# Attention tiles merged in shared PSUM banks, TensorE ordered by hand, a padded half tile and an unsplit kept relu in an attention and mixer kernel

## Chip, cores and metric

The kernel runs on one core of one Trainium2 chip. The metric is device time in microseconds from start to end of one execution. Engines: TensorE (PE) multiplies and writes only to PSUM, an accumulator memory of eight banks per partition; VectorE (DVE) and ScalarE (ACT) read PSUM and work elementwise; GpSimd (POOL) works on SBUF alone; SyncE (SP) issues the DMA transfers. A matmul has a stationary operand, loaded by its own instruction (PEld), and a moving one.

## The reference

```python
scores = scale * np.matmul(q_c, k_c.transpose(0, 1, 2, 4, 3))      # 8 x 8 heads, 9 chunks of 64, head size 64
scores = scores - np.max(scores, axis=-1, keepdims=True)
attn = np.exp(scores)
attn = attn / (np.sum(attn, axis=-1, keepdims=True) + 1e-09)
out = np.matmul(attn, v_c)
...
h = np.maximum(xt @ w_tok1, 0.0) @ w_tok2      # x: 8 batches, 576 x 512; 576 -> 256 -> 576 along the sequence
u = x + h.transpose(0, 2, 1)
h2 = np.maximum(u @ w_ch1, 0.0) @ w_ch2        # 512 -> 1536 -> 512 along the channels
return (u + h2).astype(np.float32)
```

Attention is over chunks of 64 positions. Its output, with the heads side by side, goes through a mixer: a two-layer token mix over the 576 positions, a sum, and a two-layer channel mix.

## The kernel before

**Precision.** The big products are made in a rounded form of float32. An operand is split into a high part (rounded, by ScalarE) and a low part (the rest, a subtraction), and a product is three matmuls: high by high, low weights by high, high weights by low (`THREE`). Weights arrive as raw 64-bit words; five VectorE operations and three ScalarE ones turn a block of 128x512 into its two parts (`conversion`, `split_high`, `split_low`; the result is named `kept_c1_f`, `kept_c2_f`, `kept_t...`).

**Tiles.** Two batches share nine attention tiles of 128 rows: the even batch has tiles 0 to 3 and the first half of tile 4, the odd one tiles 5 to 8 and the second half of tile 4. So an even batch attends five tiles, an odd one four. The half tile is stacked: its high part on 64 partitions and its low part on the other 64 (`attn_stack`).

**One attention tile.** `attn_s`: 16 matmuls of 64x64 in plain float32, each in two passes, so 32 in the trace, four running side by side in quarters of the array; `attn_p`: maximum and subtraction on VectorE, exponential on ScalarE; `attn_far`: transposition in blocks of 32 on VectorE, then through DRAM and back (`far`, `pf`); `attn_t`: a copy on ScalarE (`pt`); `attn_v`: 16 matmuls of 64x65 with the values, whose 65th column is all ones and gives the row sums; `attn_o`: reciprocal and product (`x`); `attn_end`: split into `xh` (ScalarE) and `xl` (GpSimd) and a second way through DRAM, whose landing in `xt` is `attn_x`. Scores and values each have the one pair of banks of `ps_at`, in turn.

**One batch of the mixer.** `tok1` (twice 14 matmuls of 128x512, of which one has 64 rows: the low weights of the half tile), its relu split into `rh` and `rl`; `tok2` (8 groups of 6 matmuls of 128x288) and the sum `u`, split into `uh` and `ul`; then for both halves of 288 columns twelve groups `ch1` (12 matmuls of 128x288, relu split into `gh` and `gl`) and twelve groups `ch2` (12 matmuls that add up in four banks, `acc`). A group of `ch2` follows the next group of `ch1`. At the end of a half the four sums are read by VectorE (`o`) and written out.

**Stages and order.** Up to about 36 us batch 0's attention runs, with PE, VectorE and ScalarE ordered by hand. Then batch 0's channel mix runs while the weights are converted: `ch1` for both halves, `ch2` for the first, the relu of the second kept split (`gh1`, `gl1`), and after it `ch2` of the second half. Batch 1's four attention tiles are placed in between by the table `JOBS`, whose slots count two per channel group. Then the main loop runs over batches 1 to 7; in batch b it attends the tiles of b+1, in pieces that a generator hands out one per channel group. In the last two stages the engines' orders are made when the program is built, by a simulated timeline with the written order as priority; only SyncE's is the written one throughout. Each engine's order is then fixed.

Of the kernel before, what the change touches and what calls it, by code (L numbers as in the profile page):

```python
# [60 lines left out]
def attention_mixer_kernel(ctx, tc, qk_in, v_in, w1_in, w2_in, wc1_in, wc2_in, out):  # L61
# [279 lines left out]
    def attn_o(i, fill=(0, 0)):  # L341
        t = tiles[i]
        pv = t["pv"]
        zi = pool.tile([P, 2, NHP, 1], F32, tag="zi", name="zi")
        nc.vector.tensor_scalar_add(out=zi, in0=pv[:, :, :, D:], scalar1=1e-9)
        convert(fill[0])
        nc.vector.reciprocal(out=zi, in_=zi)
        convert(fill[1])
# [327 lines left out]
    def jobs_of(b):  # L676
        if b >= B:
            return
        ts = batch_tiles(b)
        for j in range(len(ts) + 1):  # L680
            if j < len(ts):
                attn_s(ts[j])
                attn_p(ts[j])
                attn_far(ts[j])
                yield
                attn_t(ts[j])
            if j:
                attn_x(b, ts[j - 1])
            elif b % 2:
                attn_x(b, ts[0] - 1)  # L690
            yield
            yield
            if j < len(ts):
                attn_v(ts[j])
                attn_o(ts[j])
                attn_end(ts[j])
                if j + 2 < len(ts):
                    attn_load(ts[j + 2])
                elif b + 1 < B:
                    attn_load(batch_tiles(b + 1)[j + 2 - len(ts)])  # L700
            yield

    pend = None
    for b in range(1, B):
# [7 lines left out]
        jobs = jobs_of(b + 1)  # L712
        r = []
        for n in range(2):
            accs = []
            for f in range(NFC):
                g = ch1(us[n], f)
                end = n == 1 and f == NFC - 1
                if end:
                    for _ in jobs:  # L720
                        pass
                    if b + 1 < B:
                        r.append(tok1(b + 1, 0))
                else:
                    next(jobs, None)
# [60 lines left out]
```

## Time and profile before

| | us |
|---|---|
| three runs, median | 830.99 |
| lowest, highest | 830.38, 831.02 |
| the profiled execution | 831.2 |
| its span, first to last instruction | 829.4 |

| | busy us | share of the span |
|---|---|---|
| PE | 810.3 | 98% |
| PEld | 759.8 | 92% |
| DVE | 364.7 | 44% |
| ACT | 234.9 | 28% |
| POOL | 118.3 | 14% |

A line of a timeline has the start in us, the length in us, the engine, the line of the program, the operation and its operands with their shapes; "x12" stands for twelve instructions of a kind in a row, and a bracket at the end for idle time before the first and what ended it. A line of stretches has the stretch, its length, then busy time and instructions of PE, PEld, DVE, ACT and POOL, the clock that PE was granted, the share of busy DMA and the GB/s. A line of groups has line, engine, operation, operands and count, then total and mean time, then idle time before. Matmuls overlap, so the pace of PE is read from start to start.

### The profile page before, as it was taken

What the parts mean: (1) busy time and instruction counts of PE and PEld (TensorE: products, weight loads), DVE (VectorE), ACT (ScalarE), POOL (GpSimd) and SP (SyncE); (2) the same over time, 40 slices, a digit from 0 to 9 for tenths busy, and PEclk for the clock granted to TensorE, in tenths of its full rate; (3) what the DMA queues carried; (4) which work ended last, traced back from release to release, by engine and by line L of the source; (5) the groups of instructions that cost most, each with busy time, mean ns of one, the idle gap of its engine ahead of it and who ended that gap; (6) DMA issues with size and microseconds to landing.
All of it is one profiled execution on the core that took longest, in us unless ns stands there. A gap on an engine that the chain in (4) does not pass through costs nothing.

```text
span 829.4 us, 17900 instructions
## 1 busy us (share of the span) xinstructions
PE 810.3 (98%) x7556; PEld 759.8 (92%) x7556; DVE 364.7 (44%) x770; ACT 234.9 (28%) x484; POOL 118.3 (14%) x133
## 2 busy tenths in 40 slices
PE   7898999999999999999999999999999999999998
PEld 5578889999999999899998999999998999989998
DVE  5899993633335342343335334143433434223121
ACT  4676751322223221132223221132222322112110
POOL 0000021402103120220203102030200312014000
PEclk7999999999999999999999999999999999999999
DMA  9953232423442333023433233212353132200000
GB/s 352 407 188 102 91 103 67 144 96 96 133 121 86 120 121 122 29 75 106 131 103 99 99 113 119 65 55 90 98 162 109 62 101 92 93 24 6 1 30 29
DMA packets 69984, 87.96 MB, mean 106 GB/s; under 512 B 8016, under 2 KB 48208, under 8 KB 69904
## 3 DMA queue, kind: packets, MB, share of 16 engines
q1 hardware_dynamic: 69904, 86.82, 31.6%
q8 instruction: 59, 0.97, 0.5%
q14 instruction: 21, 0.17, 0.1%
HBM read 59.92 MB, written 25.95 MB: 104 GB/s over the span
## 4 chain that ended last, share of the span: by engine, by line
PE 88%; DVE 8%; DMA 1%; issue 1%; ACT 1%; SPq 0%; DVEq 0%; ACTq 0%
PE acc L516 36%; PE ps_c L487 34%; PE ps_t L466 6%; PE ps_t L428 6%; PE ps_s L262 3%; PE ps_v L333 2%; DVE wtop L165 1%; DVE wtop L173 1%; DVE kept_c L223 1%; DMA raw_t<-in_w 1%; DVE wtop L152 1%; DVE gl L495 1%; PE sum L437 1%; DVE wtop L158 1%; DVE mx L274 0%
## 5 line engine op out<-in xcount | busy, mean ns | idle before, releaser
L487 PE MATMUL ps_c<-uh,kept_c 128*128 128x288 f32 x1536 | 316.9, 297 | 3.4 <-ACT xt L399 1.9
L516 PE MATMUL acc<-gh,kept_c 128*128 128x288 f32 x1536 | 299.8, 297 | 0.9 <-ACT kept_c L217 0.9
L487 PEld LDWEIGHTS ps_c<-uh,kept_c 128*128 128x128 f32 x1536 | 247.2, 189 | 6.2 <-ACT xt L399 2.1
L516 PEld LDWEIGHTS acc<-gh,kept_c 128*128 128x128 f32 x1536 | 239.0, 188 | 4.5 <-ACT kept_c L217 1.1
L487 PE MATMUL ps_c<-ul,kept_c 128*128 128x288 f32 x768 | 227.8, 297 | 0.0
L495 DVE SCALAR_TENSOR_TENSOR gl<-ps_c,gh 128x288 fp32r<-128x288 f32 x192 | 87.3, 455 | 307.5 <-ACT gh L494 307.3
L516 PE MATMUL acc<-gl,kept_c 128*128 128x288 f32 x768 | 204.1, 297 | 0.0
L494 ACT ACTIVATE gh<-ps_c 128x288 fp32r<-128x288 f32 x192 | 78.9, 411 | 324.3 <-PE ps_c L487 313.3
L487 PEld LDWEIGHTS ps_c<-ul,kept_c 128*128 128x128 f32 x768 | 144.7, 189 | 0.6
L516 PEld LDWEIGHTS acc<-gl,kept_c 128*128 128x128 f32 x768 | 137.2, 189 | 1.2
L370 POOL TENSOR_TENSOR xl<-x,xh 128x512 fp32r<-128x512 f32 x28 | 36.8, 1314 | 387.8 <-ACT xh L369 387.8
L525 POOL TENSOR_TENSOR o<-o,ul 128x288 f32<-128x288 f32 x56 | 44.6, 828 | 228.9 <-DVE o L523 215.4
L466 PE MATMUL ps_t<-kept_t,rh 128*128 128x288 f32 x224 | 45.6, 301 | 0.4 <-ACT rh L445 0.4
L476 ACT CAST uh<-u 128x288 fp32r<-128x288 f32 x64 | 26.7, 432 | 46.2 <-DVE u L471 46.1
L274 DVE TENSOR_REDUCE mx<-ps_s 128x8 f32<-128x512 f32 x36 | 24.8, 688 | 29.4 <-PE ps_s L262 29.4
L466 PEld LDWEIGHTS ps_t<-kept_t,rh 128*128 128x128 f32 x224 | 35.2, 188 | 1.6 <-ACT rh L445 0.9
L314 ACT COPY pt<-pf 128x512 f32<-128x512 f32 x31 | 19.3, 622 | 60.3 <-DMA pf<-far 60.2
L428 PE MATMUL ps_t<-xh,kept_t 128*128 128x512 f32 x112 | 36.1, 403 | 0.0
L471 DVE TENSOR_TENSOR u<-ps_t,xt 128x288 f32<-128x288 f32 x64 | 28.0, 451 | 17.1 <-PE ps_t L466 16.0
L281 ACT ACTIVATE pr<-pr 128x512 f32<-128x512 f32 x36 | 22.8, 633 | 44.6 <-DVE pr L277 44.5
L477 POOL TENSOR_TENSOR ul<-u,uh 128x288 fp32r<-128x288 f32 x35 | 29.6, 855 | 20.5 <-ACT uh L476 20.1
L262 PEld LDWEIGHTS ps_s<-qk 64*64 64x64 f32 x1152 | 23.4, 138 | 9.8 <-issue 7.3
(61 smaller groups left out, 610.2 us busy)
## 6 DMA issues: line engine op xcount, KB each, us to landing
qk<-in_qk SPq DMA_DIRECT2D x36, 512.0 KB, 4.0
far<-blocks SPq DMA_DIRECT2D x63, 256.0 KB, 2.1
raw_c<-in_wc SPq DMA_DIRECT2D x24, 512.0 KB, 9.0
v<-in_v SPq DMA_DIRECT2D x36, 260.0 KB, 4.1
out<-o SPq DMA_DIRECT2D x64, 144.0 KB, 1.9
pf<-far SPq DMA_DIRECT2D x124, 64.0 KB, 2.0
xt<-far SPq DMA_DIRECT2D x112, 64.0 KB, 2.0
raw_t<-in_w SPq DMA_DIRECT2D x4, 288.0 KB, 7.6
```

What stands on the lines that cost most here:

```text
L262: nc.tensor.matmul(ps[c * CH:(c + 1) * CH, a, hp * CH:(hp + 1) * CH], lhsT=qk[a * D:(a + 1) * D, 0, hp, c * CH:(c + 1) * CH], rhs=qk[a * D ...
L370: nc.gpsimd.tensor_tensor(out=xl, in0=t["x"], in1=xh.bitcast(F32), op=ALU.subtract)
L428: nc.tensor.matmul(ps, lhsT=lhsT, rhs=rhs, start=(n == 0 and q == 0), stop=(n == len(mt) - 1 and q == len(terms) - 1),)
L466: nc.tensor.matmul(ps[:, :HALF], lhsT=lhsT[:, m * P:(m + 1) * P], rhs=rhs, start=(k == 0 and q == 0), stop=(k == NT1 - 1 and q == len(term ...
L471: nc.vector.tensor_tensor(out=u.rearrange("p (i c) -> p i c", c=BK), in0=ps[:, :HALF].rearrange("p (i c) -> p i c", c=BK), in1=xt[:, n * H ...
L476: nc.scalar.copy(out=uh[:, m], in_=u)
L477: return lambda engine: engine.tensor_tensor(out=ul[:, m], in0=u, in1=uh[:, m].bitcast(F32), op=ALU.subtract)
L487: nc.tensor.matmul(ps[:, :HALF], lhsT=weights["c1", f][:, wi, k * P:(k + 1) * P], rhs=u[ui][:, k], start=(k == 0 and q == 0), stop=(k == N ...
L494: nc.scalar.activation(out=gh, in_=ps[:, :HALF], func=AF.Relu)
L495: nc.vector.scalar_tensor_tensor(out=gl, in0=ps[:, :HALF], scalar=0.0, in1=gh.bitcast(F32), op0=ALU.max, op1=ALU.subtract)
L516: nc.tensor.matmul(accs[e], lhsT=weights["c2", f][:, wi, e * P:(e + 1) * P], rhs=g[gi], start=(f == 0 and q == 0), stop=(f == NFC - 1 and ...
L525: nc.gpsimd.tensor_tensor(out=o, in0=o, in1=u[1][:, e].bitcast(F32), op=ALU.add)
```

## The change

Four edits, and tables of numbers to go with them.

1. In the main loop the score matmuls of one tile and the value matmuls of the tile before it are issued together (`attn_both`), into the two halves of one pair of banks (`ps_sv`). The value matmuls leave out the column of ones; the row sums are now a reduction of the probabilities on VectorE (`attn_z`). `attention(k)` issues all of a step, and the steps stand at channel groups 19, 15, 11, 7 and 3 of a batch, or 19, 14, 9 and 4, with one more at group 0 of batch 1.
2. PE's order in the main loop is the written one (`manual_schedule`).
3. The half tile's low weights are kept in two copies of 128 rows, each zero in one half (`half_low`, made with `half_mask`), so that all matmuls of `tok1` have 128 rows. Batch 0's first token mix stays as it was.
4. The kept relu of batch 0's second half is one float32 tile (`g1`); it is split by a copy and a subtraction one group ahead of its use (`split_g`).

`JOBS` puts batch 1's attention two or more slots earlier and the split of the token weights two later, weights are fetched six blocks ahead instead of five, and three buffers hold low words instead of four.

```diff
-AHEAD = 5
+LAST_STEP, STRIDE, FIRST_STEP = 19, {5: 4, 4: 5}, 0
+AHEAD = 6
...
-STARTS = ((10, 11, 13, 14), (15, 16, 18, 19), (20, 21, 24, 25), (25, 27, 30, 31))
+STARTS = ((8, 9, 11, 12), (13, 14, 16, 17), (18, 19, 21, 22), (23, 24, 26, 27))
...
-JOBS += [(25 + i, "split", i) for i in range(7)]
+JOBS += [(27 + i, "split", i) for i in range(7)]
...
-        lows[i] = pool.tile([P, DM], I32, tag="low", name="low", bufs=4)[:, :n]
+        lows[i] = pool.tile([P, DM], I32, tag="low", name="low", bufs=3)[:, :n]
...
+    def attn_z(i):
+        t = tiles[i]
+        zi = t["zi"] = pool.tile([P, 2, NHP, 1], F32, tag="zs", name="zs")
+        nc.vector.tensor_reduce(
+            out=zi, in_=t["pr"].rearrange("p (h a k) -> p a h k", a=2, k=CH), axis=AX.X, op=ALU.add
+        )
+        nc.vector.tensor_scalar_add(out=zi, in0=zi, scalar1=1e-9)
+        nc.vector.reciprocal(out=zi, in_=zi)
+    def attn_both(i, j):
+        ps = ps_at.tile([P, 2, 512], F32, tag="at", name="ps_sv")
...
+                            ps[c * CH:(c + 1) * CH, a, hp * CH:(hp + 1) * CH],
+                            lhsT=qk[a * D:(a + 1) * D, 0, hp, c * CH:(c + 1) * CH],
+                            rhs=qk[a * D:(a + 1) * D, 1, hp, c * CH:(c + 1) * CH],
...
+                            ps[c * CH:(c + 1) * CH, a, (NHP + hp) * D:(NHP + hp + 1) * D],
+                            lhsT=t["pt"][a * CH:(a + 1) * CH, hp, c * CH:(c + 1) * CH],
+                            rhs=t["v"][a * CH:(a + 1) * CH, c, hp, :D],
...
-            terms = ((w[:, 0], st), (w[rows, 1], st[rows]))
+            terms = ((w[:, 0], st), (half_low[b % 2][:, m * P:(m + 1) * P], st))
...
+        if kept:
+            g = pool.tile([P, HALF], F32, tag="g1", name="g1", bufs=NFC)
+            nc.scalar.activation(out=g, in_=ps[:, :HALF], func=AF.Relu)
+            return g
...
+    def split_g(g):
+        gh, gl = g_parts()
+        nc.scalar.copy(out=gh, in_=g)
+        nc.vector.tensor_tensor(out=gl, in0=g, in1=gh.bitcast(F32), op=ALU.subtract)
+        return gh, gl
...
+        g, ahead = ahead, split_g(kept[f + 1]) if f + 1 < NFC else None
+        ch2(0, 1, us[1], f, g, accs)
...
+    def attention(k):
+        i = order[k] if k < len(order) else None
+        j = order[k - 1] if k else None
+        if j is not None:
+            attn_t(j)
+        attn_both(i, j)
+        if j is not None and k + 1 < len(order):
+            attn_load(order[k + 1])
+        if i is not None:
+            attn_p(i)
+            attn_far(i)
+            attn_z(i)
+        if j is not None:
+            attn_o(j)
+            attn_end(j)
...
+    by_hand.enter_context(tc.manual_schedule(engines={nc.tensor.engine}))
```

Three places in the built orders show what moved. Numbers behind names count the tiles of the program; a row stands for as many matmuls as its last "x" says.

PE in the main loop, before: the start of a batch's token mix (`ps_t2`), in which the scores of the next tile (`ps_s`) are spread.

```order
L262 MATMUL ps_s_8306<-qk_7800 64x64 x10
L466 MATMUL ps_t2_8199<-kept_t2_0_0_1999,rh_8134 128x288 x2
L466 MATMUL ps_t2_8199<-kept_t2_0_0_1999,rl_8135 128x288
L466 MATMUL ps_t2_8199<-kept_t2_1_0_2017,rh_8165 128x288 x2
L466 MATMUL ps_t2_8210<-kept_t2_0_0_1999,rh_8134 128x288 x2
L466 MATMUL ps_t2_8210<-kept_t2_0_0_1999,rl_8135 128x288
L466 MATMUL ps_t2_8210<-kept_t2_1_0_2017,rh_8165 128x288 x2
L262 MATMUL ps_s_8306<-qk_7800 64x64 x3
L466 MATMUL ps_t2_8199<-kept_t2_1_0_2017,rl_8166 128x288
L466 MATMUL ps_t2_8210<-kept_t2_1_0_2017,rl_8166 128x288
L262 MATMUL ps_s_8306<-qk_7800 64x64 x2
```

PE in the main loop, of the change: an attention step behind a `ch1` group (`ps_c1`) and ahead of a `ch2` group (`acc`).

```order
L535 MATMUL ps_c1_4373<-uh_3547,kept_c1_7_1215 128x288 x2
L535 MATMUL ps_c1_4373<-ul_3548,kept_c1_7_1215 128x288
L309 MATMUL ps_sv_4392<-qk_4209 64x64 x16
L321 MATMUL ps_sv_4392<-v_3975,pt_4390 64x64 x16
L575 MATMUL acc_4141<-gh_4357,kept_c2_6_1246 128x288 x2
L575 MATMUL acc_4141<-gl_4358,kept_c2_6_1246 128x288
```

Scores and values stand together and between whole groups. From the first `tok2` matmul of batch 1 on, PE has 71 runs of such small matmuls before and 28 of the change, with 864 small matmuls in both.

PE at the hand-over from batch 0 to the main loop, before: the last tile's values (`ps_v`), batch 1's token mix (`ps_t1`), a `ch2` group, and the end of the token mix, which needs the last tile (`xh_2074`, `xl_2075`).

```order
L333 MATMUL ps_v_2034<-v_1682,pt_2032 64x65 x16
L428 MATMUL ps_t1_2147<-xh_1411,kept_t1_0_2_1936 128x512
L428 MATMUL ps_t1_2147<-xl_1412,kept_t1_0_2_1936 128x512
...
L516 MATMUL acc_1847<-gh_1803,kept_c2_11_1664 128x288 x2
L516 MATMUL acc_1847<-gl_1804,kept_c2_11_1664 128x288
...
L428 MATMUL ps_t1_2116<-xh_2074,kept_t1_2_2_1954 128x512 x2
L428 MATMUL ps_t1_2147<-xh_2074,kept_t1_2_2_1954 128x512 x2
L428 MATMUL ps_t1_2116<-xl_2075,kept_t1_2_2_1954 128x512
```

The same place of the change.

```order
L575 MATMUL acc_1896<-gl_2165,kept_c2_11_1687 128x288
L575 MATMUL acc_1897<-gl_2165,kept_c2_11_1687 128x288
L379 MATMUL ps_v_1953<-v_1597,pt_1951 64x65 x16
L476 MATMUL ps_t1_2145<-xh_1991,kept_t1_2_2_2028 128x512 x2
L476 MATMUL ps_t1_2180<-xh_1991,kept_t1_2_2_2028 128x512 x2
L476 MATMUL ps_t1_2145<-xl_1992,kept_t1_2_2_2028 128x512
L476 MATMUL ps_t1_2180<-xl_1992,kept_t1_2_2_2028 128x512
L514 MATMUL ps_t2_2239<-kept_t2_0_0_2076,rh_2160 128x288 x2
```

The values and the token matmuls that need them now follow each other.

VectorE at the same hand-over, before: from batch 0's first four output sums (`o`) to the third tile's row sums (`zi`).

```order
L523 TENSOR_TENSOR o_1843<-acc_904,uh_669 128x288
L223 TENSOR_TENSOR kept_t1_0_2_1936<-wtop_257,kept_t1_0_2_1936 128x512
L223 TENSOR_TENSOR kept_t1_2_2_1954<-wtop_286,kept_t1_2_2_1954 128x512
L223 TENSOR_TENSOR kept_t1_4_1_1981<-wtop_354,kept_t1_4_1_1981 128x256
L223 TENSOR_TENSOR kept_t2_0_0_1999<-wtop_374,kept_t2_0_0_1999 128x288
L223 TENSOR_TENSOR kept_t2_1_0_2017<-wtop_379,kept_t2_1_0_2017 128x288
L223 TENSOR_TENSOR kept_t2_0_1_2059<-wtop_452,kept_t2_0_1_2059 128x288
L223 TENSOR_TENSOR kept_t2_1_1_2089<-wtop_457,kept_t2_1_1_2089 128x288
L345 TENSOR_SCALAR zi_1882<-ps_v_1865 128x8
```

Of the change: from the last tile's transpose (`blocks_1910`) to the low part of a relu of the second half (`gl_2165`).

```order
L332 STREAM_TRANSPOSE blocks_1910<-pr_1843 128x4x4x32
L231 TENSOR_TENSOR kept_t1_0_2_2006<-wtop_263,kept_t1_0_2_2006 128x512
L231 TENSOR_TENSOR kept_t1_2_2_2028<-wtop_292,kept_t1_2_2_2028 128x512
L231 TENSOR_TENSOR kept_t1_4_1_2050<-wtop_360,kept_t1_4_1_2050 128x256
L231 TENSOR_TENSOR kept_t2_0_0_2076<-wtop_380,kept_t2_0_0_2076 128x288
L231 TENSOR_TENSOR kept_t2_1_0_2098<-wtop_385,kept_t2_1_0_2098 128x288
L701 TENSOR_SCALAR half_low0_2053<-kept_t1_4_1_2050,half_mask_81 128x256
L701 TENSOR_SCALAR half_low1_2055<-kept_t1_4_1_2050,half_mask_81 128x256
L231 TENSOR_TENSOR kept_t2_0_1_2120<-wtop_458,kept_t2_0_1_2120 128x288
L231 TENSOR_TENSOR kept_t2_1_1_2142<-wtop_463,kept_t2_1_1_2142 128x288
L556 TENSOR_TENSOR gl_2165<-g1_1822,gh_2164 128x288
```

The seven low halves of the token weights stood ahead of the third tile's row sums. Now they stand, with the two masked copies, behind the last tile's transpose.

More of the change, by code (lines that the diff above doesn't have):

```diff
@@ L108, in warm @@
                 nc.tensor.matmul(ps[:, :HALF], lhsT=warm_in[:, :P], rhs=warm_in, start=True, stop=True)
+    half_mask = const.tile([P, 2], F32, name="half_mask")
+    for c in range(2):
+        nc.gpsimd.memset(half_mask[:, c:c + 1], 0.0)
+        nc.gpsimd.memset(half_mask[c * CH:(c + 1) * CH, c:c + 1], 1.0)
+    half_low = []
     weights, tops, lows = {}, {}, {}
@@ L343, in attn_o @@
         pv = t["pv"]
[L344 to L348, printed above, removed]
+        zi = t.get("zi")
+        if zi is None:
+            zi = pool.tile([P, 2, NHP, 1], F32, tag="zi", name="zi")
+            nc.vector.tensor_scalar_add(out=zi, in0=pv[:, :, :, D:], scalar1=1e-9)
+            convert(fill[0])
+            nc.vector.reciprocal(out=zi, in_=zi)
+            convert(fill[1])
         x = t["x"] = pool.tile(
@@ L497, in ch1, with g_parts @@
         )
+        return gh, gl
+    def g_parts():
+        return [pool.tile([P, HALF], F32R, tag=tag, name=tag) for tag in ("gh", "gl")]
+    def split_g(g):
+        gh, gl = g_parts()
+        nc.scalar.copy(out=gh, in_=g)
+        nc.vector.tensor_tensor(out=gl, in0=g, in1=gh.bitcast(F32), op=ALU.subtract)
         return gh, gl
@@ L638, in split @@
             split_low(i)
+            if plan[i][0][0] == "t1" and ("t1", 4) in weights and not half_low:
+                for c in range(2):
+                    kept_half = const.tile([P, DT], F32R, name=f"half_low{c}")
+                    nc.vector.tensor_scalar(
+                        out=kept_half, in0=weights["t1", 4][:, 1].bitcast(F32),
+                        scalar1=half_mask[:, c:c + 1], scalar2=None, op0=ALU.mult,
+                    )
+                    half_low.append(kept_half)
     last_of = {}
@@ L665, in attention_mixer_kernel @@
     last_of.update({i.engine: i for i in nc.cur_bb.bb.instructions})
-    accs = []
+    accs, ahead = [], split_g(kept[0])
     for f in range(NFC):
@@ L674, in attention_mixer_kernel @@
     attn_load(batch_tiles(2)[1])
[L676 to L703, printed above, removed]
+    order = [t for b in range(2, B) for t in batch_tiles(b)]
+    def attention(k):
[6 more added lines that the diff above has]
+            attn_load(order[k + 1])
+        if i is not None:
+            attn_p(i)
+            attn_far(i)
+            attn_z(i)
+        if j is not None:
+            attn_o(j)
+            attn_end(j)
+            for b in range(2, B):
+                if j in [t for t, _, _ in mix_tiles(b)] and (b % 2 == 0 or j % NTILE != 4):
+                    attn_x(b, j)
+    pend, done = None, 0
+    by_hand.enter_context(tc.manual_schedule(engines={nc.tensor.engine}))
     for b in range(1, B):
@@ L711, in attention_mixer_kernel @@
                 tok2(b, r, n, m, us[n])(nc.vector if n * NDT + m in UL_ON_VECTOR else nc.gpsimd)
-        jobs = jobs_of(b + 1)
+        ends = len(batch_tiles(b + 1)) if b + 1 < B else 0
+        steps = {LAST_STEP - STRIDE[ends] * k for k in range(ends)} if ends else ()
+        if b == 1:
+            steps = {*steps, FIRST_STEP}
+        if b % 2 == 0 and ends:
+            attn_x(b + 1, batch_tiles(b)[-1])
         r = []
@@ L718, in attention_mixer_kernel @@
                 end = n == 1 and f == NFC - 1
[L719 to L725, printed above, removed]
+                if n * NFC + f in steps:
+                    attention(done)
+                    done += 1
+                if end and b + 1 < B:
+                    r.append(tok1(b + 1, 0))
                 if pend is not None:
@@ L731, in attention_mixer_kernel @@
                         r.append(tok1(b + 1, 1))
-                    with ExitStack() if b + 1 < B else tc.manual_schedule(engines={nc.tensor.engine}):
-                        ch2(*pend)
+                    ch2(*pend)
                     pend = None
+    by_hand.close()
 def kernel(q, k, v, moe_w_tok1, moe_w_tok2, moe_w_ch1, moe_w_ch2):
```

22 lines of the change are left out of this document (17 added, 5 removed).

## Prediction

> **What bounds the kernel now.** I read the page's engine rows first, then its chain of waits, then busy time by stretch, then TensorE's own timeline.
>
> ```profile
> span 829.4 us, 17900 instructions
> PE 810.3 (98%) x7556; PEld 759.8 (92%) x7556; DVE 364.7 (44%) x770; ACT 234.9 (28%) x484; POOL 118.3 (14%) x133
> PE 88%; DVE 8%; DMA 1%; issue 1%; ACT 1%; SPq 0%; DVEq 0%; ACTq 0%
> 60.00:80.00 20.00, 17.91 (x147) 17.23 (x146) 18.96 (x43) 13.00 (x26) 0.00 (x0) 0.91 0.32 111
> 80.00:100.00 20.00, 19.12 (x164) 18.19 (x163) 20.00 (x40) 13.74 (x28) 1.30 (x1) 1.00 0.29 90
> 100.00:120.00 20.00, 17.67 (x180) 16.38 (x179) 19.62 (x41) 12.23 (x24) 1.95 (x1) 1.00 0.25 84
> 120.00:140.00 20.00, 20.00 (x200) 19.05 (x199) 10.16 (x19) 3.87 (x10) 5.30 (x5) 1.00 0.31 97
> 540.00:640.00 100.00, 100.00 (x977) 95.10 (x975) 39.59 (x82) 24.81 (x51) 15.70 (x17) 1.00 0.34 106
> ```
>
> TensorE (PE) is 98% of the span and 88% of the chain. The stretches (length, then busy time of PE, weight loads, VectorE, ScalarE, GpSimd, then granted clock) show two regimes. To about 120 us VectorE is full (20.00 of 20, 19.62 of 20): it converts the weights. From 120 us on PE never rests and VectorE is 40 to 50% busy or less. There a microsecond is saved only by taking time out of PE's stream.
>
> How much time is in that stream besides the big matmuls? Their undisturbed pace, the cost of a whole block of 16 attention matmuls (32 passes), and that of a broken piece (2 passes):
>
> ```profile
> 592.08 1.60 PE acc L516 x12
> ...
> 601.89 0.29 PE L487 MATMUL ps_c<-uh,kept_c 128*128 128x288 f32 x1
> 602.11 0.69 PE L262 MATMUL ps_s<-qk 64*64 64x64 f32 x32
> 602.74 0.40 PE L487 MATMUL ps_c<-uh,kept_c 128*128 128x288 f32 x1
> 602.98 0.29 PE L487 MATMUL ps_c<-ul,kept_c 128*128 128x288 f32 x1
> ...
> 559.46 0.29 PE L487 MATMUL ps_c<-ul,kept_c 128*128 128x288 f32 x1
> 559.68 0.33 PE L333 MATMUL ps_v<-v,pt 64*64 64x65 f32 x2
> 559.94 0.93 PE L516 MATMUL acc<-gh,kept_c 128*128 128x288 f32 x5
> 560.71 0.43 PE L516 MATMUL acc<-gl,kept_c 128*128 128x288 f32 x2
> ```
>
> Starts matter here, since matmuls overlap. Twelve take 1.60 us, 0.133 each. From 601.89 to 602.98 are 1.09 us with two big matmuls in it, so the block cost 1.09 - 0.27 = 0.82 us. From 559.46 to 560.71 are 1.25 us with six, so a piece of 2 passes cost 0.45 us. Thirty more passes cost only 0.37 us, 0.0124 each: of every interruption **0.43 us is fixed**.
>
> **The change, part by part.**
>
> *Merged interruptions, hand order.* From the first second-mixing matmul of batch 1 to the end the order has 71 interruptions before, 28 after, with the same 1728 passes. At 0.43 us fixed that saves 43 x 0.43 = 18.5 us. The other end: passes 33 to 64 of a merged block have no row of their own. If each costs 0.020 us (602.11 to 602.74 over 32 passes) instead of 0.0124, 26 blocks x 32 x 0.0073 = 6.1 us come back and 12.4 are saved. I take **-16**, nearer the upper end, because the two-pass row says the cost sits in entering and leaving.
>
> *Padded half tile.* The 64-row matmul among 128-row ones:
>
> ```profile
> 337.55 0.81 PE L428 MATMUL ps_t<-stack,kept_t 128*128 128x512 f32 x2
> 338.30 0.73 PE L428 MATMUL ps_t<-xh,kept_t 128*128 128x512 f32 x2
> ...
> 339.11 0.62 PE L428 MATMUL ps_t<-xh,kept_t 128*128 128x512 f32 x2
> 339.57 0.40 PE L428 MATMUL ps_t<-xl,kept_t 128*128 128x512 f32 x1
> ```
>
> The pair on the stack (one with 128 rows, one with 64) lasts 0.75 us from start to start, the pair behind it 0.57, an undisturbed pair 0.46. So the 64-row one costs 0.29 + 0.11 = 0.40 us more than a full one. There are 12 in batches 2 to 7. Between nothing and 4.8 us I take **-4.1**, since where another size change follows anyway the 0.11 stays. The two masked copies of the low weights are made once, on VectorE, and are counted below.
>
> The Trainium skill, page "TensorEngine Tiling (Array Packing)", sections "Theoretical Speedup" and "When to Use Tiling", speaks against padding: a contraction of 64 or less should be row-tiled, for up to twice the speed. By it the term would be 0 or a loss. The rows above say the reverse for a lone 64-row matmul in a 128-row stream; the same page's "Key Properties" has the reason, a change of tiling mode drains the engine.
>
> *What hand order could cost in the main loop.* A strict order has no fill, so each wait must be covered by what stands ahead. The low part of the relu behind an attention step: VectorE now runs max, subtraction, x, transpose, row sums, transpose before it.
>
> ```profile
> L274 DVE TENSOR_REDUCE mx<-ps_s 128x8 f32<-128x512 f32 x36 | 24.8, 688 | 29.4 <-PE ps_s L262 29.4
> ...
> L286 DVE STREAM_TRANSPOSE blocks<-x 128x512 f32<-128x512 f32 x32 | 22.7, 709 | 0.8
> L495 DVE SCALAR_TENSOR_TENSOR gl<-ps_c,gh 128x288 fp32r<-128x288 f32 x192 | 87.3, 455 | 307.5 <-ACT gh L494 307.3
> ```
>
> Six operations of about 0.70 are 4.2 us (the new row sums priced as the max over the same 128x512), the low part then ends at 4.9 us with 0.2 for signals. PE needs it after two ch1 and two ch2 groups, 4 x 1.6 = 6.4 us. Covered by 1.5 us: 0. At a batch's end VectorE takes the first output sum between the two low parts of the token mix and the rest behind them; each frees its bank ahead of PE: 0. One wait is not covered. The value matmuls need the transposed probabilities, and that way takes
>
> ```profile
> 605.73 0.33 SPq L291 DMA_DIRECT2D far<-blocks  x1
> 607.80 1.76 SPq L297 DMA_DIRECT2D pf<-far  x4
> 611.23 0.62 ACT L314 COPY pt<-pf 128x512 f32<-128x512 f32 x1 [1.14 <-DMA pf<-far]
> ```
>
> from 602.74 to 611.85, 9.1 us. Steps are 4 or 5 groups of 3.2 us apart, 12.7 us or more, except the first two (0 and 3), with five groups of 1.6 = 8.0 us between, and there ScalarE has the copy behind the relu of the group just ahead. Between 0 and 2 us, once: **+1.0**.
>
> *First stage, up to the main loop.* VectorE is the bound while it converts. Up to the last converted low half its order has 234 rows before and 220 after: eleven low parts of the kept relu, one max, one subtraction and one transpose less.
>
> ```profile
> 109.10 0.68 DVE L223 TENSOR_TENSOR kept_c<-wtop,kept_c 128x512 fp32r<-128x512 f32 x1
> 109.70 0.45 DVE L495 SCALAR_TENSOR_TENSOR gl<-ps_c,gh 128x288 fp32r<-128x288 f32 x1
> 110.07 0.70 DVE L286 STREAM_TRANSPOSE blocks<-x 128x512 f32<-128x512 f32 x1
> 110.70 0.51 DVE L152 TENSOR_SCALAR wtop<-wtop 128x512 f32<-128x512 f32 x1
> ...
> 119.02 0.69 DVE L223 TENSOR_TENSOR kept_c<-wtop,kept_c 128x512 fp32r<-128x512 f32 x1 [0.38 <-ACT kept_c L217]
> ```
>
> From start to start a low part takes 0.37, the 128x512 forms 0.60 to 0.63: 11 x 0.37 + 1.8 = 5.9 us earlier than 119.7. PE is nearly as full there (19.12 of 20), so between -5.9 and 0 I take **-5**.
>
> Then comes the hand-over to batch 1, and here the new order is worse. The ten low halves and masks of the token weights now stand on VectorE behind the last tile's transpose, and the last tile's value matmuls stand directly ahead of the token matmuls that need them; before, a ch2 group of twelve lay between.
>
> ```profile
> 144.60 0.70 PE L333 MATMUL ps_v<-v,pt 64*64 64x65 f32 x32
> 145.88 0.69 DVE L352 TENSOR_TENSOR x<-ps_v,zi 128x512 f32<-128x512 f32 x1
> 599.62 0.61 ACT L369 CAST xh<-x 128x512 fp32r<-128x512 f32 x1
> 600.31 1.29 POOL L370 TENSOR_TENSOR xl<-x,xh 128x512 fp32r<-128x512 f32 x1 [0.50 <-ACT xh L369]
> 150.82 1.29 DVE L446 SCALAR_TENSOR_TENSOR rl<-ps_t,rh 128x512 fp32r<-128x512 f32 x2 [1.35 <-ACT rh L445]
> ```
>
> Value matmuls end at 145.3, x at 146.57; with 0.6 for the high part and 1.3 for the low part PE waits 2.0 us for the one and 0.5 more for the other, then 0.6 for the relu and 0.7 for its low part: 3.9 us. The mask of the low weights comes late by 1.7 us (ten operations, some 5 us by their widths at 0.6 per 512, against some 3 us of matmuls), and this gap was nearly closed before. Between 0 and 7, **+5.5**. The kept relu's later split (12 copies on ScalarE, 12 subtractions on VectorE, priced as the low part's 0.455 us on the same 128x288) lies beside ch2 groups of 1.6 us: 0, and without that cover 12 x 0.9 = 11 us. Earlier fetching (AHEAD) and three low-word buffers let ScalarE wait longer; it is busy 13.00 of 20 there, so 0.
>
> **Sum.** 829.4 - 16 - 4.1 + 1.0 - 5 + 5.5 = 810.8 us of span. The profiled execution took 831.2, 1.8 more than its span, and stands 0.2 above the median 830.99 of the three runs: **812.6 us**.
>
> **Rivals.**
> 1. *The hand-over is no worse.* If what follows the stall is filled as before, +5.5 falls away: 807. For it: the orders of VectorE and ScalarE leave PE only one long chain. Against: PE's order there shows no other work between.
> 2. *Passes, not entries, cost the time.* Then -16 becomes -12.4 or less and the half tile gives 3: 817 to 819. Against: the two-pass row.
> 3. *Slower.* If VectorE's bunch behind each of 27 attention steps reaches beyond the 6.4 us, PE stalls at every step. It begins when the bunch takes 1.5 us more than I add up; from 0.75 us beyond that on, 2.25 us over at each step, 27 x 0.75 = 20 us are lost: 833 or more. Against: VectorE is 40% busy in the row of 540 to 640 us.
> 4. *A lower clock at the hand-over.* It happened once before:
>
> ```profile
> 68.98 1.21 PE L516 MATMUL acc<-gh,kept_c 128*128 128x288 f32 x8
> 72.28 0.58 PE L333 MATMUL ps_v<-v,pt 64*64 64x65 f32 x24 [2.09 <-ACT pt L314]
> 72.40:76.20 3.80, 3.80 (x38) 3.73 (x39) 3.42 (x7) 2.96 (x7) 0.00 (x0) 0.55 0.88 345
> ```
>
> PE rested 2.09 us and then ran 3.8 us at 0.55 of its clock. The stalls of the hand-over could do the same, 3.8 x 0.45 = 1.7 us: 814.3. The Trainium skill, page "TensorE: Matmul & The Clock Gate", Part 1, asks for an idle window of about 3.4 us before the rate is halved; this trace shows the drop after 2.1 us.
>
> **How the numbers follow.** My forecast, with the clock drop or without (809 to 816): 0.60. Rival 1, with or without the full 18.5 (803 to 809): 0.19. Rival 2 (816 to 821): 0.13. Stalls in the main loop that eat part of the gain (821 to 829): 0.04; just all of it: 0.01; slower: 0.03. A measurement tells about 0.2%, 1.7 us, from no change. The range 803 to 821 leaves 0.08 out above and little below; its ends are also near the bounds: -18.5, -4.8, +1 and -5 for the first stage (rival 1) give 829.4 - 27.3 + 1.8 = 803.9, and -12.4, -3, +1 and +4 give 820.8. Faster 0.95, same 0.02, slower 0.03.
>
> **What would show it.** Right: in the main loop one merged block of 64 passes costs 1.2 to 1.45 us from start to start, no 64-row matmul is left, a batch takes some 3.4 us less, and PE's wait rows name no low part of the relu. The last converted half ends near 114 us, the first matmul of batch 1's second mixing still starts near 151. Wrong: merged blocks of 1.6 us; idle time of PE behind `gl`, `pt` or the output sums in every batch; or a main loop that starts 4 us sooner or later.

## The result, and the profile after

| | before | after |
|---|---|---|
| runs (us) | 830.38 to 832.53, median 831.0 (4 runs) | 809.07 to 811.68, median 810.65 (4 runs) |
| ratio of the times | | 0.9751, 95% interval 0.9729 to 0.9773 |
| profiled execution, its span | 831.2, 829.4 | 810.02, 808.2 |

The forecast was 812.6 (803 to 821), from a span of 810.8; the span came out 2.6 us lower. The page of after, its span and engine rows; below them the stretches of after, with the columns of the prediction's stretches:

```profile
span 808.2 us, 17939 instructions
PE 787.4 (97%) x7556; PEld 752.1 (93%) x7556; DVE 378.0 (47%) x799; ACT 240.7 (30%) x496; POOL 118.5 (15%) x137
```

```profile
80.00:100.00 20.00, 19.29 (x166) 18.19 (x165) 20.00 (x40) 14.43 (x28) 2.99 (x1) 1.00 0.37 120
100.00:120.00 20.00, 18.84 (x191) 17.76 (x190) 17.27 (x36) 9.87 (x21) 4.72 (x5) 1.00 0.21 68
...
143.00:146.50 3.50, 1.03 (x36) 0.73 (x34) 3.22 (x8) 0.62 (x1) 2.86 (x4) 0.98 0.01 2
146.50:150.00 3.50, 3.21 (x8) 2.12 (x8) 0.32 (x2) 0.93 (x2) 1.43 (x2) 0.53 0.26 94
540.00:640.00 100.00, 100.00 (x1007) 97.59 (x1006) 43.27 (x90) 26.38 (x54) 15.60 (x17) 1.00 0.34 108
```

PE has the same 7556 instructions and is busy 22.9 us less (810.3 before). The two regimes are still there: VectorE is full first (20.00 of 20, then 17.27 of 20 in the stretch to 120, in which the conversion ends), then PE. New is the hole at the hand-over: PE is busy 1.03 of 3.50 us, and then runs 3.5 us at 0.53 of its clock.

One number divides the span: the first matmul of batch 1's second token mix starts at 150.84 before and at 149.72 after. So the first stages give 1.1 us, and the main loop, from there to the end, goes from 678.6 to 658.5 us: **20.1 us of the 21.2 come from the main loop**.

A merged step of after in the timeline of TensorE, and below it a token group of 14 matmuls (its first two rows, and the first row of what follows it) with the row that ends the same group before:

```profile
547.62 0.29 PE L535 MATMUL ps_c<-ul,kept_c 128*128 128x288 f32 x1
547.84 0.69 PE L309 MATMUL ps_sv<-qk 64*64 64x64 f32 x32
548.36 0.65 PE L321 MATMUL ps_sv<-v,pt 64*64 64x64 f32 x32
548.93 0.53 PE L575 MATMUL acc<-gh,kept_c 128*128 128x288 f32 x2
549.30 0.30 PE L575 MATMUL acc<-gl,kept_c 128*128 128x288 f32 x1
...
711.60 0.39 PE L476 MATMUL ps_t<-stack,kept_t 128*128 128x512 f32 x1
711.83 0.40 PE L476 MATMUL ps_t<-stack,half_low 128*128 128x512 f32 x1
...
714.86 0.42 PE L575 MATMUL acc<-gh,kept_c 128*128 128x288 f32 x2
```

```profile
341.20 0.42 PE L516 MATMUL acc<-gl,kept_c 128*128 128x288 f32 x2
```

From 547.62 to 549.30 are 1.68 us with three big matmuls (0.40) in it: 64 passes cost **1.28 us**, within the 1.2 to 1.45 that was forecast. The token group takes 714.86 - 711.60 = 3.26 us; before it took 341.20 - 337.55 = 3.65. So a 64-row matmul cost 0.39 us more than a full one, 4.7 us for twelve.

The hand-over of after, TensorE's timeline (a bracket is idle time and what ended it):

```profile
142.72 0.69 PE L575 MATMUL acc<-gl,kept_c 128*128 128x288 f32 x4
143.34 0.70 PE L379 MATMUL ps_v<-v,pt 64*64 64x65 f32 x32
146.53 2.08 PE L476 MATMUL ps_t<-xh,kept_t 128*128 128x512 f32 x4 [2.49 <-ACT xh L417]
148.40 1.06 PE L476 MATMUL ps_t<-xl,kept_t 128*128 128x512 f32 x2
149.72 0.55 PE L514 MATMUL ps_t<-kept_t,rh 128*128 128x288 f32 x2 [0.26 <-ACT rh L493]
```

PE stands 2.49 us for the high part of the last tile, behind its values, as the prediction worked out (2.0). The four matmuls then take 1.87 us from start to start in place of 0.93, with the clock at 0.53 of its full rate.

### The profile page after: what moved, and what is told of

It is laid out like the page before. It is cut to its first block, busy times and chain, and to the rows that moved or that the text cites. A ratio compares the mean times of both kernels' runs of the same rounds, so it can differ in the third digit from the quotient of the medians.

```text
span 808.2 us, 17939 instructions
## 1 busy us (share of the span) xinstructions
PE 787.4 (97%) x7556; PEld 752.1 (93%) x7556; DVE 378.0 (47%) x799; ACT 240.7 (30%) x496; POOL 118.5 (15%) x137
## 4 chain that ended last, share of the span: by engine, by line
PE 85%; DVE 8%; DMA 3%; ACT 2%; issue 1%; SPq 0%; ACTq 0%; DVEq 0%
PE acc L575 36%; PE ps_c L535 33%; PE ps_t L476 6%; PE ps_t L514 6%; PE ps_sv L309 2%; PE ps_sv L321 2%; DVE wtop L173 1%; DVE wtop L181 1%; DMA xc<-x 1%; DVE kept_c L231 1%; DVE wtop L160 1%; DMA raw_t<-in_w 1%; DMA pf<-far 1%; DVE wtop L166 1%; PE sum L485 0%
## 5 line engine op out<-in xcount | busy, mean ns | idle before, releaser
L535 PE MATMUL ps_c<-uh,kept_c 128*128 128x288 f32 x1536 | 310.8, 295 | 3.4 <-ACT xt L447 1.9
L575 PE MATMUL acc<-gh,kept_c 128*128 128x288 f32 x1536 | 311.9, 299 | 1.6 <-ACT kept_c L225 1.1
L575 PEld LDWEIGHTS acc<-gh,kept_c 128*128 128x128 f32 x1536 | 244.2, 188 | 6.4 <-ACT kept_c L225 1.8
L545 DVE SCALAR_TENSOR_TENSOR gl<-ps_c,gh 128x288 fp32r<-128x288 f32 x180 | 81.4, 452 | 310.1 <-ACT gh L544 309.9
L575 PE MATMUL acc<-gl,kept_c 128*128 128x288 f32 x768 | 219.5, 295 | 0.0
L544 ACT ACTIVATE gh<-ps_c 128x288 fp32r<-128x288 f32 x180 | 74.1, 411 | 317.1 <-PE ps_c L535 316.6
L575 PEld LDWEIGHTS acc<-gl,kept_c 128*128 128x128 f32 x768 | 142.9, 189 | 0.1
L582 DVE TENSOR_TENSOR o<-acc,uh 128x288 f32<-128x288 f32 x56 | 22.7, 448 | 36.1 <-PE acc L575 31.5
L514 PE MATMUL ps_t<-kept_t,rl 128*128 128x288 f32 x112 | 33.2, 297 | 0.2 <-DVE rl L494 0.2
```

Of the source, the lines that this page charges most:

```text
L514: nc.tensor.matmul(ps[:, :HALF], lhsT=lhsT[:, m * P:(m + 1) * P], rhs=rhs, start=(k == 0 and q == 0), stop=(k == NT1 - 1 and q == len(term ...
L535: nc.tensor.matmul(ps[:, :HALF], lhsT=weights["c1", f][:, wi, k * P:(k + 1) * P], rhs=u[ui][:, k], start=(k == 0 and q == 0), stop=(k == N ...
L544: nc.scalar.activation(out=gh, in_=ps[:, :HALF], func=AF.Relu)
L545: nc.vector.scalar_tensor_tensor(out=gl, in0=ps[:, :HALF], scalar=0.0, in1=gh.bitcast(F32), op0=ALU.max, op1=ALU.subtract)
L575: nc.tensor.matmul(accs[e], lhsT=weights["c2", f][:, wi, e * P:(e + 1) * P], rhs=g[gi], start=(f == 0 and q == 0), stop=(f == NFC - 1 and ...
```

## Experiments

Each kernel is after with the edit shown; the last three build on one another. All were timed beside before, in sets in which before's median lies between 830.61 and 831.0. After itself was timed again only in the set of two blocks, the unpadded half tile and the relu split at once. For each, "start" is the first matmul of batch 1's second token mix in the profiled execution, "main loop" is the span less that.

| kernel | median us | ratio to before (95%) | span | start | main loop |
|---|---|---|---|---|---|
| before | 830.61 to 831.0 | 1 | 829.4 | 150.84 | 678.6 |
| after, first time | 810.65 | 0.9751 (0.9729 to 0.9773) | 808.2 | 149.72 | 658.5 |
| after, again | 811.52 | 0.9764 (0.9749 to 0.978) | 812.5 | 151.34 | 661.2 |
| steps in two blocks | 819.66 | 0.9866 (0.9846 to 0.9886) | 815.7 | 148.63 | 667.1 |
| steps in four blocks | 838.3 | 1.0095 (1.0078 to 1.0113) | 836.6 | 149.06 | 687.5 |
| PE's order by the timeline | 831.75 | 1.0018 (1.0009 to 1.0027) | 829.0 | 149.96 | 679.0 |
| half tile not padded | 816.02 | 0.9824 (0.9806 to 0.9843) | 815.7 | 150.24 | 665.5 |
| relu split at once | 809.53 | 0.9747 (0.9734 to 0.9761) | 807.5 | 149.07 | 658.4 |
| PE kept busy, first try | 812.24 | 0.9784 (0.9761 to 0.9808) | 813.4 | 152.69 | 660.8 |
| PE kept busy, second try | 810.03 | 0.9753 (0.974 to 0.9766) | 808.9 | 150.10 | 658.8 |
| last tile in a shared bank | 811.34 | 0.9768 (0.9754 to 0.9783) | 809.8 | 149.87 | 660.0 |
| the same, steps later | 809.47 | 0.9751 (0.9734 to 0.9768) | 807.5 | 148.41 | 659.1 |
| the same, new waits taken out | 805.31 | 0.9694 (0.968 to 0.9707) | 804.0 | 146.25 | 657.7 |

**After, again.** 

> The changed kernel once more, as the common reference of this set. Both theories: 810.65 us plus or minus 1.5, span 807 to 810.

Its five runs lie between 809.51 and 814.29, and the profile fell on the longest. With the first four, after's median over nine runs is 811.3. Of the 4.3 us between the spans of its two profiles, 1.6 are there when the conversion ends (its last low half starts at 114.05 and at 115.71) and 2.4 come in batch 1, which is looked at below, with the clock.

**Steps in two and in four blocks.** The step hands out its pieces, and `ch2` takes one behind each of its four sums:

```diff
-        attn_both(i, j)
+        both = attn_both
+        ps = None
+        for parts, hps in (("s", range(NHP)), ("v", range(NHP))):
+            ps = both(i, j, hps, ps, parts)
+            yield
...
-                    ch2(*pend)
+                    ch2(*pend, step)
```

With four blocks the pieces are `("s", (0, 1)), ("s", (2, 3)), ("v", (0, 1)), ("v", (2, 3))`.

> In the main loop the 64 passes of each merged step are cut in two blocks of 32, with three big matmuls between; order by hand, banks, and the order on VectorE stay. TensorE's order then has 54 interruptions in place of 28. Theory A (every interruption has a fixed price of 0.43 us): 26 steps x (2 x 0.82 - 1.28 = 0.36) = 9.4 us more, about 820. Theory B (the gain of the main loop comes from the order by hand and fewer waits, the number of interruptions does not count): 810.65 plus or minus 1.5.

> The merged step of 64 passes is cut in four blocks of 16, with three big matmuls between; order by hand and banks stay. TensorE's order has 107 interruptions of the main loop in place of 28. Theory A (0.43 us for each, 0.0124 for a pass): a block of 16 costs 0.63, a step 4 x 0.63 = 2.52 in place of 1.28, 26 x 1.24 = 32 us more, about 843, slower than before the change although its order is by hand. Theory B (the number does not count): 811 plus or minus 2.

The timeline of TensorE with four blocks, the first two of a step:

```profile
582.07 0.29 PE L536 MATMUL ps_c<-ul,kept_c 128*128 128x288 f32 x1
582.29 0.46 PE L309 MATMUL ps_sv<-qk 64*64 64x64 f32 x16
582.68 0.53 PE L576 MATMUL acc<-gh,kept_c 128*128 128x288 f32 x2
583.05 0.30 PE L576 MATMUL acc<-gl,kept_c 128*128 128x288 f32 x1
583.28 0.46 PE L309 MATMUL ps_sv<-qk 64*64 64x64 f32 x16
```

From 582.29 to 583.28 are 0.99 us with three big matmuls (0.40): a block of 16 passes costs 0.59, four of them 2.36 in place of 1.28. Over 26 steps that makes 28 us; the main loop grew by 29.0. With two blocks it grew by 8.6, where 9.4 were worked out. Batches 2 to 6 run at full clock and without a wait in all three kernels: a batch with four whole steps takes 94.32 us in after, 95.74 with two blocks (four interruptions more) and 98.62 with four (twelve more), 0.36 for each. The order is by hand in all three, and the passes are the same. So the number of interruptions has a price, and four blocks in a hand-made order are **slower than before the change**. Theory B falls.

**PE's order by the timeline.** The line that puts TensorE's main loop in the written order is left out:

```diff
-    by_hand.enter_context(tc.manual_schedule(engines={nc.tensor.engine}))
```

> The changed kernel with TensorE's order of the main loop left to the program's simulated timeline, as before the change; merged steps in shared banks, padding and unsplit relu stay. The order then has 76 interruptions in place of 28. Theory A (the price is per interruption, 0.33 to 0.36 us by the two runs with cut blocks): 48 x 0.33 to 0.36 = 16 to 17 us more, 827 to 829: shared banks alone bring nothing without the order by hand. Theory B (merging in shared banks is what pays): below 815.

The same place in TensorE's timeline shows what the generated order does to a merged step:

```profile
598.48 0.44 PE L309 MATMUL ps_sv<-qk 64*64 64x64 f32 x10
598.86 0.53 PE L575 MATMUL acc<-gh,kept_c 128*128 128x288 f32 x2
599.32 0.33 PE L309 MATMUL ps_sv<-qk 64*64 64x64 f32 x2
```

Ten passes, two big matmuls, two passes. The main loop takes 679.0 us, 20.5 more than after, for 48 interruptions more. Of that, 1.1 us belong to no interruption: batch 7, which has no attention in it, takes 88.05 us against 86.94, since without the line its last `ch2` group also leaves the written order (in before that group was in it) and its four sums end together instead of one after the other. What is left is 0.40 for each interruption. I had expected 16 to 17 by the price of the cut blocks (8.6 / 26 = 0.33 and 29.0 / 79 = 0.37). The shared banks without the order by hand, with padding and unsplit relu, bring no gain (831.75 against 830.61 of before in the same set); the order by hand is what keeps the merged steps whole.

**Half tile not padded.**

```diff
-            terms = ((w[:, 0], st), (half_low[b % 2][:, m * P:(m + 1) * P], st))
+            terms = ((w[:, 0], st), (w[rows, 1], st[rows]))
```

> The low weights of the half tile are again a 64-row matmul, without the zero-padded copy; all else as changed. Theory A (a 64-row matmul in a 128-row stream costs 0.39 us more than a full one): 12 x 0.39 = 4.7 us more, about 815.3, of which the first form of the prediction (0 to 4.8, taken 4.1) is met at its upper part. Theory B (half the rows are no dearer, or cheaper): 810.65 or up to 1 us less.

The median is 4.5 us above after's in the same set, and the periods of batches 2 to 6 grew by 0.79 to 0.95 us, each with two such matmuls: 0.42 us for one. Theory A holds. The Trainium skill, page "TensorEngine Tiling (Array Packing)", section "When to Use Tiling", would row-tile a contraction of 64; here the lone 64-row matmul between full ones is the dear form, and the measurement decides.

**Relu split at once.**

```diff
-        kept.append(ch1(us[1], f, kept=True))
+        kept.append(ch1(us[1], f, kept="parts" if f < 11 else True))
```

With "parts", `ch1` makes `gh` and `gl` at once, as before the change.

> The relu of the second half's first eleven groups is split at once again, on VectorE among the conversions (the twelfth stays unsplit for want of memory); all else as changed. Theory A (VectorE is the bound while it converts, and the eleven low parts cost 4 to 5 us there): the last converted low half ends 4 to 5 us later, near 119 us, and the time is 4 to 5 us more, about 815. Theory B (TensorE is as full there, so the lead comes from elsewhere or is lost at the hand-over anyway): the last low half ends later but the time stays within 1.5 us of 810.65.

The last converted low half on VectorE, of after and of this kernel:

```profile
114.05 0.69 DVE L231 TENSOR_TENSOR kept_c<-wtop,kept_c 128x512 fp32r<-128x512 f32 x1 [1.00 <-ACT kept_c L225]
```

```profile
118.47 0.69 DVE L231 TENSOR_TENSOR kept_c<-wtop,kept_c 128x512 fp32r<-128x512 f32 x1 [0.74 <-ACT kept_c L225]
```

And its hand-over on TensorE, with the granted clock (before the last two numbers) of the two stretches around it:

```profile
147.06 1.09 PE L476 MATMUL ps_t<-xh,kept_t 128*128 128x512 f32 x4
147.99 0.63 PE L476 MATMUL ps_t<-xl,kept_t 128*128 128x512 f32 x2
149.07 0.53 PE L514 MATMUL ps_t<-kept_t,rh 128*128 128x288 f32 x2 [0.45 <-ACT rh L493]
```

```profile
143.00:149.00 6.00, 5.62 (x30) 4.50 (x28) 2.42 (x5) 1.20 (x3) 3.68 (x5) 1.00 0.34 111
149.00:156.00 7.00, 6.73 (x47) 6.34 (x48) 5.07 (x11) 3.10 (x8) 3.22 (x5) 1.00 0.83 272
```

The conversion ends 4.4 us later, and the main loop starts no later, 149.07 against 149.72. PE had channel groups left while the last tile went through its chain, so there was no rest and no low clock. Theory B: **the lead that the unsplit relu gives VectorE is real, and after spends it on waiting.** The median is 809.53, that of after in the same set 811.52: taken by itself in after, the unsplit relu brings no time.

**PE kept busy.** Eighteen matmuls on zeros behind the last tile's values. In the first try they were twenty and wrote unused columns of the values' bank:

```diff
+            last_v[:] = [x for x in nc.cur_bb.bb.instructions if x.engine == nc.tensor.engine][-1:]
...
+    ps = ps_acc.tile([P, 512], F32, tag="acc", name="ps_w")
+    with tc.issue_after(last_v[0]):
+        for _ in range(18):
+            nc.tensor.matmul(ps[:, :HALF], lhsT=warm_in[:, :P], rhs=warm_in, start=True, stop=True)
```

> Twenty more bf16 matmuls of 128x248 behind the last tile's values write unused columns of its bank, so that TensorE does not rest in the 2.5 us of the hand-over; nothing else. The first matmul on the last tile's high part stays where it is. Theory A (the rest lowers the granted clock behind it, by 3.5 us at 0.53 in one execution and some 10 us at 0.52 in another): the clock behind the hand-over stays at 1.0, the time is 1.6 to 4 us less, 807 to 809.5, and the runs lie closer together. Theory B (the clock falls there for another reason): 811 plus or minus 1.

> The run on the low clock once more, since there the extra matmuls stood in the values' own bank and the product behind it waited for them: now eighteen bf16 matmuls of 128x288 stand behind the last tile's values and write a bank of the output sums that is free by then. Theory A (the rest of 2.5 us lowers the granted clock behind it): the clock stays at 1.0 behind the hand-over, the second mixing of batch 1 starts near 148 to 149.5, and the time is 1.6 to 3 us less than 811. Theory B (another cause): low clock as before and 811 plus or minus 1.

The first try failed in what it was to do. The product that reads the values waited for the extra matmuls too, so the rest came behind them. Its timeline, and its stretches with the clock:

```profile
145.58 2.29 PE L690 MATMUL ps_v<-warm_in 128*128 128x248 bf16 x20
149.87 1.19 PE L477 MATMUL ps_t<-xh,kept_t 128*128 128x512 f32 x4 [2.00 <-ACT xh L418]
```

```profile
149.87:151.50 1.63, 1.46 (x5) 0.94 (x6) 0.00 (x0) 0.00 (x0) 1.28 (x1) 0.93 0.43 161
151.50:158.50 7.00, 6.74 (x26) 5.79 (x26) 2.66 (x5) 2.29 (x5) 1.60 (x2) 0.53 0.60 175
```

The second try, and below it the stretch behind the rest in after's second profile, for comparison:

```profile
147.40:158.00 10.60, 9.65 (x61) 8.28 (x62) 5.62 (x13) 4.15 (x10) 4.99 (x7) 1.00 0.65 211
```

```profile
148.15:157.00 8.85, 8.59 (x28) 7.27 (x29) 2.66 (x5) 2.14 (x5) 2.99 (x4) 0.50 0.61 180
```

In the second try PE does not rest there, and the clock stays at 1.00. One profile does not settle that the rest is the cause, as the kernel with steps in two blocks shows. It has the same rest and no low clock behind it:

```profile
145.98 1.19 PE L477 MATMUL ps_t<-xh,kept_t 128*128 128x512 f32 x4 [2.49 <-ACT xh L418]
```

```profile
146.00:160.00 14.00, 13.08 (x112) 11.49 (x113) 7.80 (x16) 5.16 (x12) 5.40 (x7) 1.00 0.58 194
```

Over all profiles, PE rests 2.00 to 2.49 us at the hand-over in seven of the changed kernels; the clock falls to 0.50 there in six of them, for 3.4 to 10.2 us. In the five in which PE does not rest there it stays at 1.00. So at the hand-over the low clock came only with the rest, but not with every rest, and how long it lasts changes from one execution to the next. What it costs up to the token mix can be read from the start of the last tile's values: 6.38 us in after (143.34 to 149.72), 5.84 with the rest and the full clock (142.79 to 148.63) and 5.84 in the second try (144.26 to 150.10). That is 0.5 us, where I had expected 1.6 to 3, and the start did not come sooner, since in that execution the values stood 0.9 us later. Waits of 0.17 to 0.45 for the parts of the tile and of the relu, most of which after does not have, keep the gain so small. Behind the start the long form costs more: batch 1, from its second token mix to that of batch 2, took 100.28 us in after's second profile and 97.91 in the first. The second try's median, 810.03, is 1.3 below after's over nine runs, but its ratio to before, 0.9753, is that of after's first runs, 0.9751: a gain is not shown. The Trainium skill, page "TensorE: Matmul & The Clock Gate", Part 1, has an idle window of some 3.4 us ahead of the lower rate; the runs here show it behind a rest of 2.00 us, and once not behind 2.49, and with a length that changes from execution to execution.

**Last tile in a shared bank.** In batch 1's attention the scores of the last tile go beside the values of the third, as in the main loop, so they need not wait until that bank is read:

```diff
-STARTS = ((8, 9, 11, 12), (13, 14, 16, 17), (18, 19, 21, 22), (23, 24, 26, 27))
+STARTS = ((8, 9, 11, 12), (13, 14, 16, 17), (18, 19), (None, None, 26, 27))
...
+JOBS += [(23, "joint")]
...
+    def joint():
+        j, i = second[2], second[3]
+        attn_z(j)
+        attn_t(j)
+        attn_both(i, j)
+        attn_p(i, 1)
+        attn_far(i)
+        attn_o(j)
+        attn_end(j)
+        attn_x(1, j)
```

> In batch 1's attention the scores of the last tile stand in the bank of the third tile's values (as in the main loop) and so need not wait for that bank; its probabilities come some 4 us sooner, and the order puts the last tile's values ahead of three channel groups. Theory A (the conversion's lead of 4 to 5 us is there but is spent on waiting for the last tile): the stall of 2.5 us and the low clock behind it go, the second mixing of batch 1 starts near 146 in place of 149.7 to 151.3, and the time is 806 to 807.5. Theory B (the lead is worth nothing, as the run with the relu split at once has the same time): another wait takes the place, and the time stays within 809 to 811.

The stall and the low clock went, and the time did not. PE's waits from 120 to 153 us in this kernel:

```profile
121.59 0.69 PE L310 MATMUL ps_sv<-qk 64*64 64x64 f32 x32 [1.47 <-DMA qk<-in_qk]
135.49 1.33 PE L576 MATMUL acc<-gh,kept_c 128*128 128x288 f32 x8 [0.79 <-ACT gh L556]
137.47 0.51 PE L477 MATMUL ps_t<-stack,half_low 128*128 128x512 f32 x1 [0.66 <-DVE half_low L715]
151.42 0.41 PE L515 MATMUL ps_t<-kept_t,rl 128*128 128x288 f32 x1 [1.02 <-DVE rl L495]
152.38 0.40 PE L515 MATMUL ps_t<-kept_t,rl 128*128 128x288 f32 x1 [0.30 <-DVE rl L495]
```

Four others took their place, 4.2 us together: the scores' operands were not there yet, ScalarE made seven high halves in a row ahead of a relu, the masks came late, and VectorE read three output sums ahead of the relu's low part. Theory B, for the time.

**The same, steps later.**

```diff
-            steps = {*steps, FIRST_STEP}
+            steps = {FIRST_STEP, *(k + 1 for k in steps)}
```

> The same with batch 1's attention steps behind the first put one channel group later (0, 4, 8, 12, 16, 20 in place of 0, 3, 7, 11, 15, 19). Theory A (the first value step waits 0.5 us for the copy of the transposed probabilities and costs 2.0 in place of 1.28): 0.7 us less than the run before it. Theory B (the later last step delays batch 2's token mix): more than the run before it.

The main loop is 0.8 us shorter, 659.1 against 660.0: theory A. The rest of the 1.9 us between the medians is the earlier start, 148.41 against 149.87, with the same waits; the first 80 us differ that much between executions of one kernel (after: 149.72 and 151.34).

**The same, new waits taken out.** The operands of the last tile are fetched two slots sooner, the token weights' low halves come one by one between the relus, and the last channel group stands behind the token matmuls:

```diff
             attn_far(i)
+            if j == 1:
+                load_qk(second[3])
...
-JOBS += [(27 + i, "split", i) for i in range(7)]
+JOBS += [(25 + i, "split", i) for i in range(7)]
...
         nc.vector.tensor_tensor(out=gl, in0=g, in1=gh.bitcast(F32), op=ALU.subtract)
+        last_of.update({i.engine: i for i in nc.cur_bb.bb.instructions[-2:]})
...
-        ch2(0, 1, us[1], f, g, accs)
+        with tc.issue_after(mixed) if f == NFC - 1 else ExitStack():
+            ch2(0, 1, us[1], f, g, accs)
```

> The run with the joined bank and the later steps, with its new waits taken away: the last tile's scores are fetched two slots earlier (1.5 us of waiting for that transfer), the low halves of the token weights and the masks are split one by one between the relus from the second group on (1.8 us behind ScalarE's seven copies in a row and the masks), and the last channel group of batch 0 stands behind the token matmuls (1.6 us behind the relu's low part). Theory A (the conversion's lead of 4 to 5 us can be kept if no wait is left at the hand-over): the second mixing of batch 1 starts near 144.5 to 146, and the time is 804 to 806.5. Theory B (each wait removed lets the next one take its place): the start stays at 148 or later, the time at 809.

The hand-over of this kernel on TensorE, and the stretch before it:

```profile
140.49 0.70 PE L380 MATMUL ps_v<-v,pt 64*64 64x65 f32 x32
...
142.81 1.11 PE L477 MATMUL ps_t<-xh,kept_t 128*128 128x512 f32 x4
144.08 0.73 PE L477 MATMUL ps_t<-xl,kept_t 128*128 128x512 f32 x2 [0.17 <-POOL xl L419]
...
146.25 0.43 PE L515 MATMUL ps_t<-kept_t,rh 128*128 128x288 f32 x2
```

```profile
120.00:140.00 20.00, 20.00 (x162) 18.75 (x161) 13.09 (x31) 8.37 (x20) 2.81 (x3) 1.00 0.23 75
```

PE is full from 120 to 140 us, a channel group of twelve lies between the values and `xh`, the start is at 146.25 and the time **805.31 us, 3% below before and 0.7% below after** (809.07 to 814.29 over nine runs, 804.3 to 805.75 here). Theory A. The three edits came together, so the share of each is not shown, and whether this version needs the unsplit relu was not tried.

## Why the prediction was right, point by point

- **Merged interruptions, -16.** Right in mechanism and size; the price under it was somewhat high. The main loop lost 20.1 us; with 4.7 for the half tile and 0.7 given back at the first step (below) 16.1 are left for the interruptions, 0.37 for each of 43. The cost sits in entering and leaving: passes 33 to 64 of a block cost (1.28 - 0.82) / 32 = 0.014 us each, near the 0.0124 that I took and not the 0.020 of the other end. The fixed part is 0.36 by the cut blocks and 0.40 by the generated order, not the 0.43 that I had from one row of two passes; the 18.5 of that price was not reached, and the 16 came from choosing between two ends. Rival 2 falls. Whether the price is a drain of the engine, as the prediction has it, no run separates from another cost of changing the shape. What the prediction did not say is that the order by hand is a condition of the whole term.
- **Padded half tile, -4.1.** Right, a little small: 4.7 by the timeline, 4.5 by the run without it. The 0.11 us behind the 64-row matmul, which I counted only in part, comes back everywhere.
- **The copy at the first steps, +1.0.** Right place, 0.7 in size, in after's first value step:

```profile
167.28 0.69 PE L309 MATMUL ps_sv<-qk 64*64 64x64 f32 x32
168.47 0.70 PE L321 MATMUL ps_sv<-v,pt 64*64 64x64 f32 x32 [0.49 <-ACT pt L360]
```

  All other merged steps cost 1.28, this one 2.00; steps one group later gave 0.8 back.
- **VectorE's bunch behind each step, 0.** Right. No wait of the main loop names the low part of a channel relu (`gl`), and rival 3 did not come. PE's waits in the main loop are 0.93 us in all, at the start of batch 1: 0.26 and 0.18 for the token relu and 0.49 for the copy above.
- **First stage -5 and hand-over +5.5.** The sum was nearly right (+0.5, measured -1.1), its parts were not independent. The conversion did end 5.0 us sooner (119.7 before, 114.7 after), and the hand-over gave back 3.9. Two things were off in the 5.5, on opposite sides, so that the sum came so near is partly luck. The masks were not late, as the timelines of VectorE and TensorE in after show:

```profile
136.73 0.61 DVE L701 TENSOR_SCALAR half_low<-kept_t,half_mask 128x256 fp32r<-128x256 f32 x2
```

```profile
138.06 0.40 PE L476 MATMUL ps_t<-stack,half_low 128*128 128x512 f32 x1
```

  They were done at 137.34, and PE took the first at 138.06 with no wait; that 1.7 falls away. And the low clock, which I had as rival 4 at +1.7, did come in both profiles of after; it cost 0.5 us up to the token mix, and with the 2.4 of batch 1 some 3 in the second. Nor was such a drop a single event in before, as the prediction has it: that trace has the clock at 0.50 also from 35.3 and from 45.5 us on, behind rests of 1.84 and 1.89 us. The step that failed is taking the lead as a gain and the stall as a loss, each with its own bounds: the run with the relu split at once shows that the lead had no worth as long as the last tile's chain ends when it does, and the last version starts its main loop 3.5 us sooner than after (146.25 against 149.72), once the chain is moved. Rival 1 (no stall) falls for after, and is about what the last version does (805.3 against its 803 to 809).

## What to carry to other kernels

Count the changes of matmul shape in TensorE's order, not only the matmuls: here each run of small ones cost 0.36 to 0.40 us beside its passes, and merging paid only with an order that keeps the runs whole. A stage that ends sooner is worth what the next wait allows; price a lead and the stall behind it as one term, by following the chain that the stall waits for. When a stall goes and the time stays, list the waits that are new and take them out together.

## What the runs showed of the hardware that I had not expected

At the hand-over six profiles of the changed kernels have a rest of TensorE of 2.43 to 2.49 us. The granted clock behind it is 0.50 for 3.4 us in two of them (after, PE's order by the timeline), for 6.8 us in two (four blocks, half tile not padded), for 10.2 us in one (after, again), and it stays at 1.00 in one (two blocks). A wait of 1.47 us in the version with the shared bank had no low clock behind it either: its clock row stays at 1.00 from 120 to 165 us.

The times of after scatter by 5.2 us over nine runs, 809.07 to 814.29. In the versions without the rest they scatter by 0.6 to 2.3 us, in those with it by 1.4 to 5.2. So the low clock behind this rest is a part of the scatter and not all of it: between the two profiles of after 1.6 us lie ahead of the conversion's end, and where they come from was not followed up.
